# Where five early loads are queued, and a second MLP layer with batches on two column groups

## The chip, the cores and the metric

The kernel runs on one core of a Trainium2 chip. The metric is the device time of one execution in microseconds (us). Executions of one kernel agree within some 0.3%; the kernel before shows two groups of times, near 668.3 and near 669.7 us, in the same session. Every kernel is compared with runs of the kernel before in its own session. A ratio is the mean time of one kernel's fast runs over that of the kernel before's fast runs of the same rounds, so it is not quite the ratio of the medians quoted beside it.

## The reference

One decode step of a transformer block for 8 batches, width 512, bf16. The key and value caches (8 batches, 8 heads, 8192 x 128 each) are 268 MB of the 284 MB read.

```python
mod = silu(c) @ w_mod                    # six parts: sa, ca, ga, sb, cb, gb
h = layernorm(x) * (1 + ca) + sa
x = x + ga * attention(h, k_cache, v_cache, wq, wo)   # 32 query heads, 8 kv heads
h = layernorm(x) * (1 + cb) + sb
x = x + gb * (relu(h @ w1 + b1) ** 2 @ w2 + b2)       # 512 -> 1792 -> 512
```

## The kernel before

Each engine runs its instructions in the order in which the program adds them; semaphores tie engines together. The caches come in 64 units of 4 MB, K units and V units below, through a ring of four slots in SBUF. Code here and below is shortened: `...` marks a cut, and lines such as `a += b @ c` stand for one instruction. SyncE issues almost all loads. w_mod and wq borrow ring slots 2 and 3, so K units 2 and 3 wait until those are used. The first V unit (`n == NSLOT`) also waits for wo, which makes that wait stand in for one in front of wo's readers inside the batch loop.

```python
def load(n):
    ...
    dep = [released.get(s), d_wo if n == NSLOT else None]
    ...
    loaded[n] = dma("sync", s_ring[s], lambda e: e.dma_start(slot(s), src), dep)
...
# after the projections of mod and q:
load(0)
load(1)
dma("sync", s_bb, ... b1 ...); dma("sync", s_bb, ... b1 ...); d_bb = dma("sync", s_bb, ... b2 ...)
d_wo = dma("sync", s_wo, lambda e: e.dma_start(
    wo_sb[:, :, :].rearrange("p (g j) n -> p g (j n)", j=4),     # 8 runs of 4 KB per partition
    A_wo.rearrange("(g p j) n -> p g (j n)", g=8, p=128)))
load(2)
load(3)
```

The end, after the last V unit: w1 comes in two loads and w2 in four, all queued behind the last V unit. The first layer runs over k (4) and then f (14), so all 14 tiles finish with the last k. The second layer has the weights as stationary operand and 8 batch columns moving.

```python
for k in range(KT):
    ...
    for f in range(FT):          # 56 matmuls, 128x16 out
        hT_ps[f // 8][:, f % 8] += W1[k, f].T @ hbT[:, k]
# two halves: scale, add, squared relu on VectorE
for f in range(FT):
    for k in range(KT):          # 56 matmuls, 128x8 out
        yT_ps[:, k, :] += W2v[:, f, 128*k:128*(k+1)].T @ hidT[:, f, :]   # waits d_w2[f // 4]
k_y2 = vector: y2T = yT_ps * mod(5)
# four transposing matmuls of y2T (and four of x1T, the residual) into o_ps rows 0:8 and 64:72
# copy (VectorE one half, ScalarE the other), store from two queues
```

## Time and profile before

The median was 669.21 us over four runs (668.52 to 669.9), the three before the prediction included.

| in the trace of before | us |
|---|---|
| span, first to last instruction | 666.7 |
| first data packet | 1.8 |
| w_mod, wq, K0, K1, wo landed | 11.3, 21.0, 30.8, 41.1, 51.3 |
| K2, K3 landed | 61.6, 71.3 |
| four w2 loads landed | 660.17, 661.46, 662.69, 663.33 |
| store issued (SyncE) | 664.92 |

Landings here and below are the last of the 16 increments that the DMA engines give a load's semaphore. The prediction below shows the views that go with them. In a view, SPq and ACTq are the DMA issues of SyncE and ScalarE, PEld is a weight load of TensorE, and PEclk is the granted share of TensorE's clock.

### The profile page before, as it was taken

Reading aid. Unit: us, or ns where it says so; the run is one execution under the profiler, and the core shown is the slowest. Engines: PE = TensorE matmul, PEld = TensorE weight load, DVE = VectorE, ACT = ScalarE, POOL = GpSimd, SP = SyncE. Lnnn points to the kernel's source line nnn. Section 1 sums busy time; section 2 is a strip of 40 time slices with the busy share of each in tenths; the row PEclk is TensorE's granted clock in tenths of the full one; section 3 lists DMA queues with packets and bytes.
Section 4 is the critical chain, followed back from the end, with each engine's and each line's share of the span. In section 5 each row is a group of like instructions: output and inputs, shape, how many; then the busy total and the mean of one; then the engine's idle time right before and its main releaser. Section 6 shows DMA issues by size and latency. Waiting matters only on the chain.

```text
span 666.7 us, 15924 instructions
## 1 busy us (share of the span) xinstructions
PE 528.3 (79%) x7259; PEld 352.2 (53%) x7259; DVE 307.9 (46%) x587; ACT 264.3 (40%) x307; POOL 20.5 (3%) x79
## 2 busy tenths in 40 slices
PE   3494976898849987599858988499776998589887
PEld 2383732675328742477316753287424773277535
DVE  1262741466316652367415662167513673146633
ACT  2151631466115651166314661166512663146611
POOL 7400000000000000000000000000000000000000
PEclk9696998799969999699998999799997999879996
DMA  9999999999999999999999999999999999999997
GB/s 375 437 406 441 419 433 433 425 434 431 438 427 433 433 434 427 434 434 425 434 431 438 427 431 434 434 427 431 438 425 434 433 436 427 431 434 434 427 420 285
DMA packets 12189, 283.85 MB, mean 426 GB/s; under 512 B 1261, under 2 KB 1297, under 8 KB 3601
## 3 DMA queue, kind: packets, MB, share of 16 engines
q1 hardware_dynamic: 12128, 283.65, 99.3%
q8 instruction: 9, 0.15, 0.1%
q10 hardware_dynamic: 48, 0.02, 0.0%
q14 instruction: 4, 0.02, 0.0%
HBM read 283.66 MB, written 0.01 MB: 425 GB/s over the span
## 4 chain that ended last, share of the span: by engine, by line
PE 52%; DMA 38%; ACT 6%; DVE 2%; issue 1%; SPq 0%; DVEq 0%
PE PS L488 36%; DMA ring<-in_A_k_cache_dram 33%; PE PS L505 9%; ACT P_sb L582 5%; DMA ring<-in_A_v_cache_dram 4%; DMA ring<-in_A_wq_dram 2%; PE PS L636 2%; PE PS L478 1%; ACT KTb L493 1%; DVE O_sb L656 1%; PE PS L472 1%; PE PS L594 1%; DVE Pm L608 0%; PE PS L614 0%; PE PS L773 0%
## 5 line engine op out<-in xcount | busy, mean ns | idle before, releaser
L488 PE MATMUL PS<-IDENT,ring 128*128 128x128 bf16 x4096 | 267.1, 227 | 56.2 <-DMA ring<-in_A_k_cache_dram 56.2
L488 PEld LDWEIGHTS PS<-IDENT,ring 128*128 128x128 bf16 x4096 | 246.5, 102 | 104.8 <-DMA ring<-in_A_k_cache_dram 57.4
L493 ACT ACTIVATE KTb<-PS 128x1024 bf16<-128x1024 bf16 x192 | 196.5, 1024 | 236.6 <-PE PS L488 236.6
L495 DVE COPY KTb<-PS 128x1024 bf16<-128x1024 bf16 x320 | 210.0, 688 | 146.5 <-PE PS L488 144.4
L636 PE MATMUL PS<-ring,Pm 128*32 128x512 bf16 x1018 | 67.2, 409 | 24.8 <-DMA ring<-in_A_v_cache_dram 23.9
L505 PE MATMUL PS<-KTb,Qb 128*32 128x512 bf16 x1024 | 79.0, 385 | 4.5 <-ACT KTb L493 4.5
L656 DVE CAST O_sb<-PS 128x512 bf16<-128x512 f32 x31 | 21.5, 692 | 112.7 <-PE PS L636 112.7
L636 PEld LDWEIGHTS PS<-ring,Pm 128*32 128x32 bf16 x1018 | 26.5, 101 | 61.8 <-DMA ring<-in_A_v_cache_dram 33.7
L535 ACT ACTIVATE KTb<-PS 32x192 bf16<-32x192 f32 (+1 forms) x18 | 5.6, 310 | 110.0 <-PE PS L472 103.9
L582 ACT ACTIVATE P_sb<-PS,negm 128x1024 bf16<-128x1024 f32 x32 | 35.2, 1111 | 20.2 <-DVE negm L577 20.2
L478 PE MATMUL PS<-ONES 128*128 128x512 f32 x80 | 42.1, 630 | 0.0
L472 PE MATMUL PS<-IDENT 128*128 128x512 bf16 x112 | 33.4, 380 | 0.0
L594 PE MATMUL PS<-IDENT,P_sb 128*128 128x128 bf16 x256 | 19.9, 220 | 15.4 <-ACT P_sb L582 15.4
L608 DVE COPY Pm<-PS 64x512 bf16<-64x512 bf16 x48 | 20.2, 421 | 25.0 <-PE PS L594 24.5
L594 PEld LDWEIGHTS PS<-IDENT,P_sb 128*128 128x128 bf16 x256 | 14.4, 98 | 25.1 <-ACT P_sb L582 25.1
L505 PEld LDWEIGHTS PS<-KTb,Qb 128*32 128x32 bf16 x1024 | 15.4, 94 | 21.0 <-ACT KTb L493 8.5
L512 DVE TENSOR_REDUCE m<-PS 128x1 f32<-128x512 f32 x32 | 22.1, 689 | 6.6 <-PE PS L505 6.6
L660 PEld LDWEIGHTS PS<-SEL,O_sb 128*128 128x128 bf16 x124 | 5.8, 97 | 30.0 <-DVE O_sb L656 30.0
L478 PEld LDWEIGHTS PS<-ONES 128*128 128x128 f32 x80 | 12.7, 190 | 10.6 <-issue 10.6
L660 PE MATMUL PS<-SEL,O_sb 128*128 128x8 bf16 x124 | 7.8, 169 | 12.3 <-DVE O_sb L656 12.0
L472 PEld LDWEIGHTS PS<-IDENT 128*128 128x128 bf16 x112 | 9.9, 104 | 10.1 <-issue 7.2
L543 PE MATMUL PS<-wo_sb,KTb 128*32 128x512 bf16 x192 | 11.8, 380 | 3.3 <-ACT KTb L535 3.3
(134 smaller groups left out, 147.0 us busy)
## 6 DMA issues: line engine op xcount, KB each, us to landing
ring<-in_A_k_cache_dram SPq DMA_DIRECT2D x32, 4096.0 KB, 34.0
ring<-in_A_v_cache_dram SPq DMA_DIRECT2D x31, 4096.0 KB, 27.8
ring<-in_A_wq_dram SPq DMA_DIRECT2D x1, 4096.0 KB, 19.8
wo_sb<-in_A_wo_dram SPq DMA_DIRECT2D x1, 4096.0 KB, 47.3
ring<-in_w_mod_dram SPq DMA_DIRECT2D x1, 3072.0 KB, 10.5
ring<-in_A_v_cache_dram SPq DMA_DIRECT2D x1, 2048.0 KB, 22.5
ring<-in_B_w_dram SPq DMA_DIRECT2D x3, 512.0 KB, 19.2
ring<-in_B_w_dram SPq DMA_DIRECT2D x1, 1344.0 KB, 17.8
```

Source lines behind the costliest of these rows:

```text
L472: ts = [op("tensor", lambda e: e.matmul(bank(at).rearrange("p (a r) -> p a r", a=4), IDENT[:, :], rhs)) for _ in range(n)]
L478: ts = [op("tensor", lambda e: e.matmul(bank(at).rearrange("p (a r) -> p a r", a=4), ONES[:, :], rhs)) for _ in range(n)]
L488: t = op("tensor", lambda e, j=j, i=i: e.matmul(STG[j][:, i, :], src[:, 32 * k + 8 * j + i, :], IDENT[:, :], is_transpose=True), [loaded[n ...
L493: stg_free[j] = op("scalar", lambda e, j=j, dst=dst: e.activation(dst, STG[j], ACT.Copy), [t])
L495: stg_free[j] = op("vector", lambda e, j=j, dst=dst: e.tensor_copy(dst, STG[j]), [t])
L505: t = op("tensor", lambda e, hf=hf, q=q, rhs=rhs: e.matmul(PS[32 * q:32 * (q + 1), k, :], Qb[:, 2 * p + hf, :], rhs, start=(p == 0 and hf ...
L512: return op("vector", lambda e: e.tensor_reduce(m4[:, k:k + 1], bank(k), AX.X, ALU.max), [t])
L582: exps.append(op("scalar", lambda e, k=k: e.activation(P_sb[:, k, :, :, :], bank(k).rearrange("p (i x) -> p i x", i=8).unsqueeze(2).to_bro ...
L594: t = op("tensor", lambda e, k=k, i=i: e.matmul(STG[k][:, i, :], P_sb[:, k, i, :, :].rearrange("p h x -> p (h x)"), IDENT[:, :], is_transp ...
L608: done.append(op("vector", lambda e, dst=dst, frm=frm: e.tensor_copy(dst, frm), [t, k_pm]))
L636: t = op("tensor", lambda e, m=m, cg=cg, p=p, vt=vt, Obank=Obank: e.matmul(Obank[32 * cg:32 * (cg + 1), :], lhs[:, p, 32 * m:32 * m + 32], ...
L656: t = op("vector", lambda e, osb=osb, Obank=Obank: e.tensor_copy(osb, Obank), [t])
```

## The change

Its intent was to shorten the end and to relieve SyncE and GpSimd. The first layer is done for tiles 0 to 7 and then 8 to 13, so that the second can begin early. The second layer swaps its operands: the batches are stationary, 256 columns of w2 move, on two column groups of the array; the result then lies in rows as the output wants it, so the gate, the residual and the store follow without transposes. ScalarE issues five of the early loads. GpSimd builds its constants with fewer instructions.

```diff
+        for q in range(4):
+            op("vector", ... mod5[32 * q:32 * (q + 1), :] <- mod_r[96:128, 1, ...])
         load(0)
-        load(1)
-        dma("sync", s_bb, ... b1 ...)
+        load(1, "scalar")
+        dma("scalar", s_bb, ... b1 ...)          # and the other two bias loads
-        d_wo = dma("sync", s_wo, lambda e: e.dma_start(
+        d_wo = dma("scalar", s_wo, lambda e: e.dma_start(
...
+        # beside the mean: x1_ps rows 0:8 and 64:72 <- x1T transposed; later two ScalarE copies to x1_sb
-        for k in range(KT):
-            for f in range(FT):
+        for hh, (fa, fz) in enumerate(((0, 8), (8, FT))):
+            for k in range(KT):
+                for f in range(fa, fz):
...
         for f in range(FT):
-            for k in range(KT):
-                yT_ps[:, k, :], W2v[:, f, k * 128:(k + 1) * 128], hidT[:, f, :]
+            for cc in range(2):
+                y_ps[64 * cc:64 * cc + B, :], hidT[:, f, :], W2v[:, f, 256 * cc:256 * (cc + 1)],
+                    tile_position=(0, 64 * cc)
-        k_y2 = vector: y2T = yT_ps * mod(5);  transposes;  copies
+        vector: y_sb = y_ps * mod5
+        vector: out_sb = y_sb + x1_sb
...
-        # GpSimd: 7 selects for R4, 4 for R4m, 32 for SEL
+        # GpSimd: 4 selects for R4, one scaled copy for R4m, 4 for SEL
```

More of the change, by code (lines that the diff above doesn't have):

```diff
@@ L225, in bass_adaLN_cond__gqa_block_cached__dense_activation_squared_relu__decode_kernel @@
         cb1 = sb("cb1", [128, KT, B], FP32)
-        b_row = sb("b_row", [4, 512 + 128], BF16)
-        SELB = sb("SELB", [4, 4, B], BF16)
+        b_row = sb("b_row", [4, 512 + 256], BF16)
+        SELB = sb("SELB", [4, 4, 32], BF16)
         SELP = sb("SELP", [128, B], FP32)
         x1T = sb("x1T", [128, KT, B], BF16)
+        x1_sb = sb("x1_sb", [128, 256], BF16)
+        mod5 = sb("mod5", [128, 256], FP32)
         sqs = sb("sqs", [128, B], FP32)
@@ L256, in bass_adaLN_cond__gqa_block_cached__dense_activation_squared_relu__decode_kernel @@
         proj = KF[:, 4096:5120].bitcast(FP32)
-        b1_row, b2_row = b_row[:, 0:512], b_row[:, 512:640]
-        y2T = KF[:, 0:KT * B].rearrange("p (k b) -> p k b", k=KT)
+        b1_row, b2_row = b_row[:, 0:512], b_row[:, 512:768]
+        y_sb = KF[:, 5120:5376]
         rT = KF[:, 1024:1024 + 2 * FT * B].bitcast(FP32).rearrange("p (f b) -> p f b", f=FT)
@@ L301, in bass_adaLN_cond__gqa_block_cached__dense_activation_squared_relu__decode_kernel @@
         pool(lambda e: e.memset(Qmask[:], 1.0))
-        pool(lambda e: e.memset(R4m[:], 0.0))
+        pool(lambda e: e.memset(x1_sb[:], 0.0))
         pool(lambda e: e.memset(SEL[:], 0.0))
@@ L325, in bass_adaLN_cond__gqa_block_cached__dense_activation_squared_relu__decode_kernel @@
         k_pm = t
-        for d in (-96, -64, -32, 0, 32, 64, 96):
-            t = select(R4[:], [[-1, 128]], -d, 1, 1.0, NE, t)
+        for d in (0, 32, 64, 96):
+            t = select(R4[:].rearrange("p (a r) -> p a r", a=4), [[0, 4], [-1, 32]], -d, 1, 1.0, NE, t)
         t = select(Qmask[:], [[-32, 4]], 0, 1, 0.0, GE, t)
         t = select(Qmask[:], [[32, 4]], 31, -1, 0.0, GE, t)
-        for d in (0, 32, 64, 96):
-            t = select(R4m[:], [[-1, 32]], -d, 1, 0.5, NE, t)
-        for i in range(4):
-            for cg in range(4):
-                for half in range(2):
-                    t = select(SEL[:, i, 4 * half:4 * half + 4], [[-1, 4]], -(32 * cg + 8 * i + 4 * half), 1,
-                               1.0, NE, t)
+        t = pool(lambda e: e.tensor_scalar(R4m[:], R4[:, 0:32], 0.5, None, ALU.mult), [t])
+        for cg in range(4):
+            t = select(SEL[:], [[-8, 4], [-1, 8]], -32 * cg, 1, 1.0, NE, t)
         t = pool(lambda e: e.memset(SELP[:], 0.0), [t])
@@ L342, in bass_adaLN_cond__gqa_block_cached__dense_activation_squared_relu__decode_kernel @@
         t = select(PERM[:], [[-1, 4], [0, 4], [-4, 32]], 0, 1, 1.0, NE, t)
-        t = select(SELB[:], [[-1, 4], [0, B]], 0, 1, 1.0, NE, t)
+        t = select(SELB[:], [[-1, 4], [0, 32]], 0, 1, 1.0, NE, t)
         t = pool(lambda e: e.memset(oTn[:], 0.0), [t])
@@ L353, in bass_adaLN_cond__gqa_block_cached__dense_activation_squared_relu__decode_kernel, with load @@
         F2 = FT - 2
-        def load(n):
+        def load(n, eng="sync"):
             kv, b, p = units[n]
@@ L368, in load @@
             else:
-                loaded[n] = dma("sync", s_ring[s], lambda e: e.dma_start(slot(s), src), dep)
+                loaded[n] = dma(eng, s_ring[s], lambda e: e.dma_start(slot(s), src), dep)
         k_sig = op("scalar", lambda e: e.activation(sig, c_sb, ACT.Sigmoid), [d_c])
@@ L449, in bass_adaLN_cond__gqa_block_cached__dense_activation_squared_relu__decode_kernel @@
         k_cb1 = op("vector", lambda e: e.tensor_scalar(cb1[:], mod(4), 1.0, None, ALU.add))
+        for q in range(4):
+            op("vector", lambda e, q=q: e.tensor_copy(
+                mod5[32 * q:32 * (q + 1), :], mod_r[96:128, 1, 256 * (q // 2):256 * (q // 2 + 1)]), [k_mr1])
         stg_free = [k_modT, None, None, k_QTm]
@@ L453, in bass_adaLN_cond__gqa_block_cached__dense_activation_squared_relu__decode_kernel @@
         load(0)
-        load(1)
-        dma("sync", s_bb, lambda e: e.dma_start(
+        load(1, "scalar")
+        dma("scalar", s_bb, lambda e: e.dma_start(
             b1_row[0:3, :], B_b1[0:128 * F2].rearrange("(o f) -> o f", o=3)), [k_brow])
-        dma("sync", s_bb, lambda e: e.dma_start(
+        dma("scalar", s_bb, lambda e: e.dma_start(
             b1_row[3:4, 0:256], B_b1[128 * F2:F].rearrange("(o f) -> o f", o=1)))
-        d_bb = dma("sync", s_bb, lambda e: e.dma_start(b2_row, B_b2.rearrange("(o f) -> o f", o=4)))
-        d_wo = dma("sync", s_wo, lambda e: e.dma_start(
+        d_bb = dma("scalar", s_bb, lambda e: e.dma_start(b2_row[0:4:2, :], B_b2.rearrange("(o f) -> o f", o=2)))
+        d_wo = dma("scalar", s_wo, lambda e: e.dma_start(
             wo_sb[:, :, :].rearrange("p (g j) n -> p g (j n)", j=4),
@@ L516, in bass_adaLN_cond__gqa_block_cached__dense_activation_squared_relu__decode_kernel @@
         hT_ps = [bank(i)[:, 0:16 * n].rearrange("p (f a b) -> p f a b", f=n, a=2) for i, n in enumerate((8, FT - 8))]
-        yT_ps = bank(2)[:, 0:KT * B].rearrange("p (k b) -> p k b", k=KT)
+        y_ps = bank(2)[:, 0:256]
         def permute(pP, q0, q1, dst, deps, fill, then=None):
@@ L706, in bass_adaLN_cond__gqa_block_cached__dense_activation_squared_relu__decode_kernel @@
                             op("tensor", lambda e, hh=min(hh, 1), f0=f0 + j, j=j, n=n, a=a, z=z: e.matmul(
-                                hT_ps[hh][:, f0:f0 + 4 * (z - a - 1) + 1:4, 1, :], brow(j, n), SELB[:, a:z, :],
+                                hT_ps[hh][:, f0:f0 + 4 * (z - a - 1) + 1:4, 1, :], brow(j, n), SELB[:, a:z, 0:B],
                                 start=(f0 == 0), stop=False, skip_group_check=True), [d_bb, s_bank_free[min(hh, 1)]])
                     op("tensor", lambda e: e.matmul(
-                        yT_ps, b2_row, SELB[:, :, :], start=True, stop=False, skip_group_check=True),
+                        y_ps, SELB[:, :, :].rearrange("o a r -> o (a r)"), b2_row, start=True, stop=False, skip_group_check=True),
                         [s_bank_free[2]])
@@ L741, in bass_adaLN_cond__gqa_block_cached__dense_activation_squared_relu__decode_kernel @@
                                                     stop=(k == KT - 1)), [k_x1])
+        x1_ps = bank(7)[:, 0:256]
+        for cc in range(2):
+            rows = slice(64 * cc, 64 * cc + B)
+            for k in range(2):
+                t1 = op("tensor", lambda e, rows=rows, k=k, cc=cc: e.matmul(
+                    x1_ps[rows, 128 * k:128 * (k + 1)], x1T[:, 2 * cc + k, :], IDENT[:, :],
+                    tile_position=(0, 64 * cc)), [k_x1])
         bc = lambda ap: ap.unsqueeze(1).to_broadcast([128, KT, B])
@@ L751, in bass_adaLN_cond__gqa_block_cached__dense_activation_squared_relu__decode_kernel @@
         rsb = lambda n: rstd2[:].unsqueeze(1).to_broadcast([128, n, B])
-        for k in range(KT):
-            if k == KT - 1:
-                t = op("tensor", lambda e: e.matmul(var_ps, ONESM[:, :], sqs[:]), [k_sqs])
-                t = op("scalar", lambda e: e.activation(std2[:], var_ps, ACT.Sqrt, bias=epst[:, 0:1]), [t])
-                k_rstd = op("vector", lambda e: e.reciprocal(rstd2[:], std2[:]), [t])
-            for f in range(FT):
-                t = op("tensor", lambda e, f=f, k=k: e.matmul(
-                    hT_ps[f // 8][:, f % 8, :, :], wcol(k, f), hbT[:, k, :, :], start=False, stop=(k == KT - 1),
-                    skip_group_check=True), [k_hb, k_sb, d_w1[k // (KT - 1)]])
-                if k == KT - 1 and f in (7, FT - 1):
-                    hh = f // 8
-                    fs = slice(8 * hh, f + 1)
-                    t = op("vector", lambda e, hh=hh, fs=fs: e.tensor_tensor(
-                        rT[:, fs, :], hT_ps[hh][:, :, 0, :], rsb(fs.stop - fs.start), ALU.mult), [t, k_rstd])
-                    t = op("vector", lambda e, hh=hh, fs=fs: e.tensor_tensor(
-                        rT[:, fs, :], rT[:, fs, :], hT_ps[hh][:, :, 1, :], ALU.add), [t])
-                    k_sq.append(op("vector", lambda e, fs=fs: e.scalar_tensor_tensor(
-                        hidT[:, fs, :], rT[:, fs, :], 0.0, rT[:, fs, :], ALU.max, ALU.mult), [t]))
@@ L770, in bass_adaLN_cond__gqa_block_cached__dense_activation_squared_relu__decode_kernel @@
-        o_ps = bank(4)[:, 0:256]
-        for f in range(FT):
-            for k in range(KT):
-                t = op("tensor", lambda e, f=f, k=k: e.matmul(
-                    yT_ps[:, k, :], W2v[:, f, k * 128:(k + 1) * 128], hidT[:, f, :],
-                    start=False, stop=(f == FT - 1), skip_group_check=True), [k_sq[f // 8], d_w2[f // 4]])
-        for cc in range(2):
-            for k in range(2):
-                op("tensor", lambda e, k=k, cc=cc: e.matmul(
-                    o_ps[64 * cc:64 * cc + B, 128 * k:128 * (k + 1)], x1T[:, 2 * cc + k, :], IDENT[:, :],
-                    start=(k == 0), stop=False, tile_position=(0, 64 * cc), skip_group_check=True), [k_x1])
@@ L781, in bass_adaLN_cond__gqa_block_cached__dense_activation_squared_relu__decode_kernel @@
-        k_y2 = op("vector", lambda e: e.tensor_tensor(y2T, yT_ps, mod(5), ALU.mult), [t])
-        outf = out.rearrange("b s d -> (b s) d")
-        d_o = []
-        for cc in (1, 0):
-            for k in range(2):
-                t = op("tensor", lambda e, k=k, cc=cc: e.matmul(
-                    o_ps[64 * cc:64 * cc + B, 128 * k:128 * (k + 1)], y2T[:, 2 * cc + k, :], IDENT[:, :],
-                    start=False, stop=(k == 1), tile_position=(0, 64 * cc), skip_group_check=True), [k_y2])
-            rows = slice(64 * cc, 64 * cc + B)
-            if cc == 0:
-                t = op("vector", lambda e, rows=rows: e.tensor_copy(out_sb[rows, :], o_ps[rows, :]), [t])
-            else:
-                t = op("scalar", lambda e, rows=rows: e.activation(out_sb[rows, :], o_ps[rows, :], ACT.Copy), [t])
-            d_o.append(dma(("sync", "scalar")[cc], s_out[cc], lambda e, cc=cc, rows=rows: e.dma_start(
-                outf[:, 256 * cc:256 * (cc + 1)], out_sb[rows, :]), [t]))
+        for hh, (fa, fz) in enumerate(((0, 8), (8, FT))):
+            for k in range(KT):
+                if (hh, k) == (0, 2):
+                    t = op("tensor", lambda e: e.matmul(var_ps, ONESM[:, :], sqs[:]), [k_sqs])
+                    t = op("scalar", lambda e: e.activation(std2[:], var_ps, ACT.Sqrt, bias=epst[:, 0:1]), [t])
+                    k_rstd = op("vector", lambda e: e.reciprocal(rstd2[:], std2[:]), [t])
+                    for rows in (slice(0, B), slice(64, 64 + B)):
+                        k_res = op("scalar", lambda e, rows=rows: e.activation(
+                            x1_sb[rows, :], x1_ps[rows, :], ACT.Copy), [t1])
+                for f in range(fa, fz):
+                    t = op("tensor", lambda e, f=f, k=k: e.matmul(
+                        hT_ps[f // 8][:, f % 8, :, :], wcol(k, f), hbT[:, k, :, :], start=False, stop=(k == KT - 1),
+                        skip_group_check=True), [k_hb, k_sb, d_w1[k // (KT - 1)]])
+            fs = slice(fa, fz)
+            t = op("vector", lambda e, hh=hh, fs=fs: e.tensor_tensor(
+                rT[:, fs, :], hT_ps[hh][:, :, 0, :], rsb(fs.stop - fs.start), ALU.mult), [t, k_rstd])
+            t = op("vector", lambda e, hh=hh, fs=fs: e.tensor_tensor(
+                rT[:, fs, :], rT[:, fs, :], hT_ps[hh][:, :, 1, :], ALU.add), [t])
+            k_sq.append(op("vector", lambda e, fs=fs: e.scalar_tensor_tensor(
+                hidT[:, fs, :], rT[:, fs, :], 0.0, rT[:, fs, :], ALU.max, ALU.mult), [t]))
@@ new lines, in bass_adaLN_cond__gqa_block_cached__dense_activation_squared_relu__decode_kernel @@
+        for f in range(FT):
+            for cc in range(2):
+                t = op("tensor", lambda e, f=f, cc=cc: e.matmul(
+                    y_ps[64 * cc:64 * cc + B, :], hidT[:, f, :], W2v[:, f, 256 * cc:256 * (cc + 1)],
+                    start=False, stop=(f == FT - 1), tile_position=(0, 64 * cc), skip_group_check=True),
+                    [k_sq[f // 8], d_w2[f // 4]])
+        t = op("vector", lambda e: e.tensor_tensor(y_sb, y_ps, mod5[:], ALU.mult), [t])
+        t = op("vector", lambda e: e.tensor_tensor(out_sb, y_sb, x1_sb[:], ALU.add), [t, k_res])
@@ L796, in bass_adaLN_cond__gqa_block_cached__dense_activation_squared_relu__decode_kernel @@
+        outf = out.rearrange("b s d -> (b s) d")
+        d_o = [dma(eng, s_out[cc], lambda e, cc=cc: e.dma_start(
+            outf[:, 256 * cc:256 * (cc + 1)], out_sb[64 * cc:64 * cc + B, :]), [t])
+            for cc, eng in enumerate(("sync", "scalar"))]
         Pg.wait("sync", d_o)
```

## The prediction

> **What bounds the kernel now.** I read the page first, for what is busy all the time:
>
> ```profile
> DMA  9999999999999999999999999999999999999997
> GB/s 375 437 406 441 419 433 433 425 434 431 438 427 433 433 434 427 434 434 425 434 431 438 427 431 434 434 427 431 438 425 434 433 436 427 431 434 434 427 420 285
> ```
>
> All 16 DMA engines are busy from the first slice to the last, at some 430 GB/s: 283.65 MB have to pass. No compute engine is full (PE 79%, DVE 46%). In the packet records of the trace 15 or more packets are in flight for 658 of the 666.7 us, and none for only 2.8 us, nearly all of it before the first packet (1.8 us) and after the last. So the time is three terms: 1.8 us until data flows, one unbroken stream, and what follows its last byte. A change can move the time only by tearing a hole into the stream or by altering the end.
>
> The second view is the timeline, SyncE's early issues and then the tail. Columns are start, length, engine, line, operation.
>
> ```profile
> 0.80 0.39 SPq L287 DMA_DIRECT2D ring<-in_w_mod_dram  x1
> 1.25 0.42 SPq L289 DMA_DIRECT2D ring<-in_A_wq_dram  x1
> 1.72 1.26 SPq L369 DMA_DIRECT2D ring<-in_A_k_cache_dram  x2
> 4.00 0.40 SPq L460 DMA_DIRECT2D wo_sb<-in_A_wo_dram  x1
> 14.86 23.69 SPq L369 DMA_DIRECT2D ring<-in_A_k_cache_dram  x2
> 51.38 31.83 SPq L369 DMA_DIRECT2D ring<-in_A_v_cache_dram  x4
> ```
>
> By 4.4 us five big loads (w_mod, wq, two K units, wo) stand in one queue, and they land in that order: 11.3, 21.0, 30.8, 41.1 and 51.3 us. The first V load waits for wo (51.38, just after it landed), but two more K units stand behind wo and keep the engines busy until 71. The wait costs nothing.
>
> ```profile
> 660.88 0.23 DVE L764 TENSOR_TENSOR KTb<-PS,rstd 128x64 f32<-128x64 f32 x1
> 661.68 2.06 PE L773 MATMUL PS<-KTb,ring 128*128 128x8 bf16 x56 [1.00 <-DVE KTb L768]
> 663.78 0.19 DVE L781 TENSOR_TENSOR KTb<-PS,modT 128x32 bf16<-128x32 f32 x1 [1.56 <-PE PS L773]
> 664.03 0.38 PE L786 MATMUL PS<-IDENT,KTb 128*8 128x128 bf16 x4
> 664.49 0.41 DVE L791 CAST KTb<-PS 8x256 bf16<-8x256 f32 x1 [0.51 <-PE PS L786]
> 664.92 0.31 SPq L794 DMA_DIRECT2D out_dram<-KTb  x1
> ```
>
> The chain of waits puts this tail down to PE and DVE. The landings say otherwise. The four w2 loads, by the semaphore events, land at 660.17, 661.46, 662.69 and 663.33 us, and the second-layer matmuls stop and start with them: tiles 8 to 11 begin at 662.83, the last two at 663.37. So the weights, not the first layer, set when the second layer ends.
>
> ```profile
> L682 SPq DMA_DIRECT2D ring<-in_B_w_dram x4: 885/1444/5533, 641.0 to 649.9; - x4
> DMA to landing us min/median/max: 13.5/17.0/19.2
> ```
>
> The last is issued at 649.9 and lands 13.5 us later: 663.4. After it come 8 matmuls, a multiply, 4 transposes, a copy and the store. The granted clock is 0.5 from 656.2 us to the end.
>
> **What the Trainium skill says.** *DMA: Bandwidth & Descriptors*, "Queues, rings and completion order": SP and ACT each own one ring on each of the same 16 engines, and an engine goes round-robin between rings by packet. The trace agrees. The load of x (ScalarE's queue, 1 KB packets), issued at 1.44 among 24 KB packets of w_mod, starts its packets only at 5.4 to 6.8 us, behind about four; and in all eight pairs (matched in order of time) its 4-byte completion packet starts 0.95 us after the data packet, about one 24 KB packet (0.92 to 1.0 us), against 0.04 us for the load of c, while nothing competes. Small packets pay one large one per turn. The same page, "Issuing engines are not separate DMA queues": a second issuer saves issue time alone. *TensorEngine Tiling (Array Packing)*, "Key Properties": column tiles run in parallel. This trace agrees: 32 matmuls of 512 columns on four column groups took 3.60 us at clock 0.53, 8 rounds of 0.45 us, and 24 of which eight used two groups took 3.42, again 8 rounds. *VectorE: DVE Perf Modes* (table of caps by operand): a tensor_tensor with a PSUM operand runs at 1x. Here 128x512 from PSUM took 0.69 us and 128x64 0.23, so some 0.43 for 256 columns.
>
> **The change part by part.**
> *Set-up on GpSimd.* It loses 3 of 7 wide selects, 4 small and 28 of 32 tiny ones (29 of them took 9.48 us). GpSimd now ends at 29.4 us and the first K unit lands at 30.8, so the 10 us saved are hidden. Four 32x256 copies on DVE (mod5) are added near 27 us, some 1.5 us, about the same place and hidden. Worth 0.
>
> *Five loads on ScalarE.* A queue is in program order: in the new order these loads stand behind the activation that copies q, which runs at 24.81 to 25.41. So K unit 1, the biases and wo go out at about 25.4 to 28 us instead of 2 to 4.4. Meanwhile SyncE holds w_mod, wq, K0 (to 30), K2 (issued at 14.86 with room in the queue) and K3 (about 24.8). No hole there. But now two rings compete. Per engine a 4 MB K unit is 8 packets of 32 KB (1.217 us each), wo is 64 of 4 KB (0.164 each). K1 starts behind about four packets, near 31, then alternates with K2: both end near 31 + 16 x 1.217 = 50.5. Then K3 alternates with wo, one packet each: 7 to 8 turns x 1.38 = 10 us, so K3 ends near 61 with only 8 of wo's 64 packets moved. The other 56 take 9.2 us: wo's data ends near 70, **last of all**. The first V load, which has to wait for it, and all loads behind it in SyncE's queue find the stream empty. The hole: 0.42 us from last data to landing (x: 7.75 to 8.13), 0.08 to issue, 1.04 to first packets (0.80 to 1.84 at the start), some 0.8 as first packets are slow (1.5 to 2.4 us against 0.92 later), and part of the spread of the engines' landings (1.7 us), since the slowest gates all: 2.3 + 0.3 = **+2.6 us**. PE has K1 at 51 instead of 41, but ends K3 near 81 as now near 83; slots 1 and 2 are released by about 70.
>
> *First layer half by half.* Lets the second layer begin at about 660.8 (32 of 56 matmuls, 1.2 us after 658.28, then three DVE operations of 0.77) instead of 661.68. That is 0.9 us gained which the w2 landings take back: tiles 8 to 11 still begin at 662.83. Worth 0.
>
> *Second layer with batches on two column groups.* 56 matmuls of 8 columns (32 ns each) become 28 of 256. At half clock a pair takes 256/1.2 GHz = 0.213 us (scaled from the 0.45 us round). Tiles 8 to 11: 662.83 + 0.85 = 663.68; the last two + 0.43, and 0.1 to 0.15 until the result is there: 664.2, against 663.78 before. **+0.45 us**. At full clock it would be near 663.75: 0.
>
> *Gate and residual.* Removed after the matmuls: multiply, transposes back and copy, 663.78 to 664.90 = 1.12 us. Added: a 128x256 multiply (0.43) and an add (0.43 or less) with a gap of 0.03: 0.89. **-0.25 us**. The residual's transposes move into PE's idle time near 657.9, and their two copies to ScalarE's near 660.
>
> Sum: 0 + 2.6 + 0 + 0.45 - 0.25 = +2.8 us.
>
> **Rivals.**
> *(a) wo comes in time.* If the rings share by bytes, wo lands near 66, before K3 ends near 70, and there is no hole: 669.8. Against it are the x packets above. For it: x shows one packet per turn, not a long run.
> *(b) The end gains after all.* If tiles and half clock are not as supposed, the tail may save up to 0.8 us as the author wanted: 669 with (a). Against it are the w2 landings.
> *(c) The column groups serialize,* or the weight load of each pair shows: +0.85 us or more behind the last two landings, 673 to 674. Against it are the two rounds above.
> *(d) ScalarE blocks in issuing wo,* as SyncE's load at 14.86 blocked until 37.5 behind wo. It would stall the copies of K0, which has slack; 0 to +0.5.
>
> **Range and chances.** The hole I hold 85% likely. With it 672.4 with 0.9 either way; without it 669.3 to 670.2. Weighted I say **672.2 us, 670.2 to 673.8**. Two per cent are 13 us, and neither the stream's bytes nor its rate change: same 0.97, slower 0.02, faster 0.01.
>
> **What would show it.** In the new profile: wo landing near 71, after K3, and the next V issue right after; a dip of the DMA share near 70 to 73; K1 landing near 50. In the tail: second layer starting some 0.9 us earlier against the last landing, but ending 0.8 us behind it, its matmuls pausing for w2. The prediction is wrong if wo lands before K3, if the DMA share has no dip, or if the matmuls of the second layer take 1.7 us or more per four tiles.

## The result, and the profile after

The changed kernel takes 672.9 us (672.61 to 673.1, 4 runs) against 669.21: ratio 1.0055, 95% interval 1.0037 to 1.0072. It is 3.7 us slower, inside the two per cent that count as the same, but clear of noise.

The page of the changed kernel, rows of DMA share and rate:

```profile
DMA  9999899999999999999999999999999999999996
GB/s 374 433 426 412 336 430 436 433 435 431 424 431 437 433 433 426 430 433 433 437 431 422 431 437 433 435 428 426 433 435 435 431 430 426 435 433 435 428 416 263
```

One slice, the fifth (67 to 84 us), has fallen from 419 to 336 GB/s. Nothing else of that size has changed in the middle. The timeline of the changed kernel, SyncE's issues and then ScalarE's early ones, shows what stands around it:

```profile
1.73 23.16 SPq L367 DMA_DIRECT2D ring<-in_A_k_cache_dram  x3
71.40 8.97 SPq L367 DMA_DIRECT2D ring<-in_A_v_cache_dram  x4
...
24.57 0.60 ACT L430 ACTIVATE KTb<-PS 128x512 bf16<-128x512 f32 x1 [8.76 <-PE PS L400]
24.58 0.38 ACTq L367 DMA_DIRECT2D ring<-in_A_k_cache_dram  x1
26.37 0.40 ACTq L461 DMA_DIRECT2D wo_sb<-in_A_wo_dram  x1
```

SyncE's first V load went out at 51.38 before; now it goes out at 71.40. wo, issued at 26.37, landed at 71.32, last of all; K1, K2 and K3 had landed at 49.62, 50.83 and 62.84. SyncE's waits, before and then after, name it (columns: total us, times, longest):

```profile
SPq L116 <- DMA wo_sb<-in_A_wo_dram: 12.7, 1, 12.7
```

```profile
SPq L116 <- DMA wo_sb<-in_A_wo_dram: 46.4, 1, 46.4
```

The wait before cost nothing, since two K units were still queued behind wo. The stretches around 70 us, first before and then after (length, busy us and count of PE, PEld, DVE, ACT, POOL, then clock, DMA share, GB/s), show that the longer one does. A packet is counted whole in the stretch in which it starts, so a share can pass 1:

```profile
68.00:70.00 2.00, 2.00 (x37) 1.63 (x30) 1.09 (x3) 1.48 (x2) 0.00 (x0) 1.00 0.87 369
70.00:72.00 2.00, 2.00 (x37) 1.47 (x33) 1.30 (x3) 1.03 (x2) 0.00 (x0) 1.00 0.97 410
72.00:74.00 2.00, 2.00 (x36) 1.47 (x34) 1.29 (x3) 1.52 (x2) 0.00 (x0) 1.00 1.21 524
```

```profile
68.00:70.00 2.00, 2.00 (x40) 1.88 (x40) 1.30 (x3) 1.05 (x2) 0.00 (x0) 1.00 0.58 229
70.00:72.00 2.00, 2.00 (x37) 1.59 (x30) 1.10 (x3) 1.48 (x2) 0.00 (x0) 1.00 0.03 12
72.00:74.00 2.00, 2.00 (x36) 1.47 (x34) 1.30 (x3) 1.03 (x2) 0.00 (x0) 1.00 0.98 270
```

PE is full in both, and at full clock: no compute engine shows the loss. Only the DMA share does. Summed over the packet records of the two load queues between 65 and 80 us, the 16 engines stand still for 3.35 us on average after and 0.12 before. This stretch is called the hole below.

The end of the changed kernel, in the timeline:

```profile
664.08 0.23 DVE L774 TENSOR_TENSOR KTb<-PS,rstd 128x64 f32<-128x64 f32 x1
664.87 3.43 PE L782 MATMUL PS<-ring,KTb 128*8 128x256 bf16 x28 [0.16 <-DVE KTb L778]
666.82 0.97 PEld L782 LDWEIGHTS PS<-ring,KTb 128*8 128x8 bf16 x12 [0.58 <-issue]
668.34 0.42 DVE L786 TENSOR_TENSOR KTb<-PS,mod 128x256 bf16<-128x256 f32 x1 [2.91 <-PE PS L782]
668.80 0.29 DVE L787 TENSOR_TENSOR KTb<-KTb,x_sb 128x256 bf16<-128x256 bf16 x1
669.12 0.37 SPq L789 DMA_DIRECT2D out_dram<-KTb  x1
```

The four w2 loads landed at 664.19, 665.48, 666.72 and 667.35. Each event is best read against the last of them, since the hole has shifted everything. The second layer starts 2.48 us ahead of it (1.65 before), so the first layer by halves does what it was meant to. But the matmuls pause until the third load has landed, and run on to 0.95 us behind the last (0.42 before). The store is issued 1.77 us behind it, 1.59 before.

### The profile page after: what moved, and what is told of

Its sections match the earlier page's. It is cut to its first block, busy times and chain, and to the rows that moved or that the text cites. A ratio compares the mean times of both kernels' runs of the same rounds, so it can differ in the third digit from the quotient of the medians.

```text
span 671.4 us, 15797 instructions
## 1 busy us (share of the span) xinstructions
PE 530.9 (79%) x7227; PEld 353.1 (53%) x7227; DVE 309.9 (46%) x591; ACT 264.7 (39%) x308; POOL 14.7 (2%) x45
## 4 chain that ended last, share of the span: by engine, by line
PE 54%; DMA 37%; ACT 6%; DVE 2%; issue 1%; SPq 0%; DVEq 0%
PE PS L489 37%; DMA ring<-in_A_k_cache_dram 30%; PE PS L506 10%; ACT P_sb L583 5%; DMA ring<-in_A_v_cache_dram 4%; DMA ring<-in_A_wq_dram 3%; PE PS L637 2%; PE PS L479 1%; ACT KTb L494 1%; DVE O_sb L657 1%; PE PS L473 1%; PE PS L595 1%; PE PS L400 1%; PE PS L782 0%; DVE Pm L609 0%
## 5 line engine op out<-in xcount | busy, mean ns | idle before, releaser
L494 ACT ACTIVATE KTb<-PS 128x1024 bf16<-128x1024 bf16 x192 | 196.7, 1024 | 230.3 <-PE PS L489 230.3
```

What stands on the lines that cost most here:

```text
L494: stg_free[j] = op("scalar", lambda e, j=j, dst=dst: e.activation(dst, STG[j], ACT.Copy), [t])
```

## The experiments

Eight kernels, all with correct results. The first four of the table's eight were timed in five rounds in one session (kernel before: 668.28, nine runs), the other four in three rounds in another (669.44, seven runs).

| kernel | median us | ratio to before (95%) | wo landed | idle DMA, 65 to 80 us |
|---|---|---|---|---|
| changed | 672.90 | 1.0055 (1.0037 to 1.0072) | 71.3 | 3.35 |
| changed, loads back | 668.95 | 1.0010 (0.9996 to 1.0024) | 51.9 | 0.12 |
| changed, wo alone back | 668.75 | 1.0003 (0.9989 to 1.0017) | 51.2 | 0.12 |
| loads back, four groups | 669.07 | 1.0006 (0.9992 to 1.0019) | 51.8 | 0.07 |
| before, halves only | 668.49 | 0.9998 (0.9984 to 1.0011) | 51.1 | 0.12 |
| before, five loads moved | 672.52 | 1.0046 (1.0029 to 1.0063) | 71.2 | 3.35 |
| before, wo alone moved | 672.21 | 1.0042 (1.0025 to 1.0058) | 71.2 | 3.19 |
| changed, loads issued at the start | 672.86 | 1.0051 (1.0034 to 1.0068) | 71.3 | 3.34 |
| changed, wait moved to the third V load | 672.84 | 1.0053 (1.0036 to 1.0070) | 90.6 | 0.12 (3.08 from 80 to 100) |

A packet is one piece that one DMA engine moves, as the trace records it. My theory, H: two queues share each DMA engine by turns of one packet, so wo with its 4 KB packets is starved by units with 32 KB packets, lands last, and the V load that waits for it finds the stream empty. The rivals: T, the new second layer costs the time; K, the late second K unit does, by delaying PE and the slots; L, the loads are merely issued too late.

**The five loads, undone and alone.** In the changed kernel:

```diff
-        load(1, "scalar")
+        load(1)
-        dma("scalar", s_bb, ...)     # three, and d_wo
+        dma("sync", s_bb, ...)
```

> The changed kernel with its five early loads (second K unit, three bias rows, wo) back on SyncE in the old place; everything else of the change stays. Theory H (the hole: wo lands last, about 70 us, because two rings alternate packet by packet, and the first V load waits for it): wo lands near 51 again, the 3.2 us of idle DMA engine time between 65 and 80 us go to 0.1, and the time is the kernel before's plus the tail's 0.2: 669.4 us, ratio to before 1.000 (0.999 to 1.001). Rival T (the second layer with 256 columns at half clock costs the time): stays near 672, ratio 1.004.

It came to 1.0010: the hole is gone (0.12 us idle, wo at 51.9) and so is the loss, but for at most the tail. The opposite edit, in the kernel before:

> The kernel before with only the five loads moved to ScalarE, all else old. Theory H: the whole loss is here: wo lands near 71 us after the fourth K unit, 3.2 us of idle DMA engine time near 70, 672.4 us, ratio 1.0048. Rival T (the tail): ratio 1.000.

It came to 1.0046. The two add up to the whole change: 0.0010 + 0.0046 against 0.0055. T falls as the cause of the loss; a small cost of the tail, up to 0.0024 by the interval of the first, stays possible.

**wo alone, undone and alone.** In the changed kernel and, turned round, in the kernel before:

```diff
-        d_wo = dma("scalar", s_wo, ...
+        d_wo = dma("sync", s_wo, ...
```

> The changed kernel with wo alone moved back to SyncE's queue, behind the first K unit; the second K unit and the bias rows stay late on ScalarE. Theory H: wo lands by about 52 us, no hole near 70, 669.4 us, ratio 1.000 though the second K unit still lands late, at 41 to 50. Rival K (the late second K unit delays PE and with it all slot releases): stays at 672.5 to 673, ratio 1.005.

> The kernel before with only the load of wo moved to ScalarE, which comes to it at about 25 us. Theory H: three K units stand on SyncE's queue, wo's small packets get one turn to each of theirs, wo lands last near 70 to 71 and the hole is the same: 672.4 us, ratio 1.0048. Rival K (the late second K unit): it is early here, so no loss, ratio 1.000.

With wo back the ratio is 1.0003, with the second K unit and the biases still on ScalarE and that unit issued at 24.60; it landed at 41.98, though, nearly as early as before. With wo alone moved, the loss is there in full, 1.0042, though the second K unit landed at 42.7. In the two kernels SyncE's first V issues stand as far apart as in before and after (first wo back, then wo alone moved):

```profile
51.25 31.79 SPq L367 DMA_DIRECT2D ring<-in_A_v_cache_dram  x4
```

```profile
71.32 4.27 SPq L369 DMA_DIRECT2D ring<-in_A_v_cache_dram  x4
```

So one load in one place is the whole cause of the hole, and K falls as its explanation: the second K unit is early in the kernel that loses. That a K unit at 50 us would be harmless by itself was not run; in neither of these two did it come that late.

**Late, or on the other queue?** The five loads stay on ScalarE but stand ahead of its first activation:

```diff
+        load(1, "scalar")            # and the biases and wo, as they were
         k_sig = op("scalar", lambda e: e.activation(sig, c_sb, ACT.Sigmoid), [d_c])
...
         load(0)
-        load(1, "scalar")            # and the biases and wo
         load(2)
```

> The changed kernel with the five loads still on ScalarE but issued at the very start, before its first activation. Theory H (two rings by turns of one packet, 4 KB against 32 KB): w_mod is held up by the second K unit to 18 or 20 us, wo is starved by wq and the K units and still lands last, 66 to 71 us; the hole stays for the most part: 671.5 to 673, ratio 1.003 to 1.006. Rival L (only the late issue at 25 us does harm): no hole, ratio 1.000.

wo was issued at 4.47 us, nearly as early as in the kernel before (4.00), and landed at 71.32; w_mod at 18.8 instead of 11.3, wq at 31.9. Ratio 1.0051. L falls: with these two queues, issuing early does not help.

The packet records confirm the turns in numbers. In this kernel 439 of wo's 1024 packets had started by 60 us: 27 per engine, one for each of the 8 large packets of wq, of K0 and of K2, and three of K3. In the kernel with wo alone moved it was 416, 26 per engine; in the changed kernel, where wo comes behind the second K unit, 150, some 9 per engine. There, from 50 to 58 us, 94 packets of wo started beside 93 of SyncE's K units, though each of the latter is eight times as large.

One more rival is that ScalarE's queue as such is served less. The second K unit in the changed kernel speaks against it: it was on that queue too, with packets of 32 KB, and from 32 to 46 us 89 of them started beside 89 on SyncE's queue. A load of wo in larger packets, which would test the size alone, was not run.

**What if the load does not wait?** The wait for wo moves to the third V load, whose landing still comes ahead of wo's first reader:

```diff
-            dep = [released.get(s), d_wo if n == NSLOT else None]
+            dep = [released.get(s), d_wo if n == NSLOT + 2 else None]
```

> The changed kernel with the wait for wo moved from the first V load of the first batch to the third (wo is first read after the third has landed). Theory H: nothing is idle near 70 any more, but the first two V units join SyncE's queue and starve wo for 16 more turns: it lands last at 88 to 91 us, and the third V load then finds the stream empty: the hole moves to near 90 and the time stays, 672 to 673, ratio 1.004 to 1.006. Rival: if wo gets a fair share of bytes once the wait is gone, it lands by 80, no hole, ratio 1.000.

The ratio is 1.0053 and the hole has moved along: SyncE issued the first V unit at 43.96, wo, starved for 16 more turns, landed at 90.59, and the stretches around 90 us of this kernel look like those around 70 of the changed one:

```profile
86.00:88.00 2.00, 1.13 (x16) 0.79 (x14) 1.20 (x3) 2.00 (x5) 0.00 (x0) 1.00 1.00 399
88.00:90.00 2.00, 1.45 (x18) 1.11 (x19) 1.07 (x4) 1.68 (x4) 0.00 (x0) 1.00 0.38 154
90.00:92.00 2.00, 1.69 (x15) 0.61 (x16) 0.91 (x4) 0.63 (x2) 0.00 (x0) 1.00 0.84 231
```

As long as the other queue has large packets, wo is served one small packet per turn, and whoever waits for it waits until the other queue is dry. Wait and starvation together make the hole.

**The halves alone.** The kernel before with the changed first layer and nothing else:

> The kernel before with only the first layer by halves; second layer, output transposes and loads as before. My step: the second layer starts some 0.9 us earlier against the last weight landing, but tiles 8 to 11 still begin 0.13 us after the third w2 load landed and the last two after the fourth, so the time stays: ratio 1.000 (0.9990 to 1.0005). Rival: the first layer is on the path and 0.8 us are saved, ratio 0.9988.

Ratio 0.9998. The second layer of this kernel, in the timeline:

```profile
660.80 1.23 PE L772 MATMUL PS<-KTb,ring 128*128 128x8 bf16 x32 [0.18 <-DVE KTb L767]
662.76 0.93 PE L772 MATMUL PS<-KTb,ring 128*128 128x8 bf16 x24 [0.73 <-DMA ring<-in_B_w_dram]
664.87 0.31 SPq L793 DMA_DIRECT2D out_dram<-KTb  x1
```

It starts 2.46 us ahead of the last w2 landing (663.26) instead of 1.65, does 32 matmuls, and then waits 0.73 us for the third w2 load. The store is issued 1.61 us behind the last landing, against 1.59. What was gained went into waiting for the weights.

**A tail with four column groups.** With the loads back, the second layer on four groups of 128 columns, tried as a version that might beat both kernels:

```diff
-            for cc in range(2):      # y_ps[64*cc: +8, 0:256] on column group 64*cc
+            for cc in range(4):      # y_ps[32*cc: +8, 0:128] on column group 32*cc
...
-        two stores of 8x256, one per queue
+        four stores of 8x128, two per queue
```

> Loads on SyncE as in the kernel before, first layer by halves, and the second layer on four column groups of 128 columns instead of two of 256; gate and residual on 128x128; four stores of 2 KB, two per queue. If column groups run side by side, each pair of tiles after the last weights takes half: second layer ends 0.3 to 0.4 us earlier against the last landing than in the changed kernel, gate and add together 0.50 instead of 0.71, one more store issue in each queue +0.3: in all 0.2 to 0.4 below the run with the loads back, 669.0 us, ratio 0.9990 to 0.9998. If groups serialize: nothing gained in the matmuls, ratio 1.000 or more.

Its tail, in the timeline; the last w2 load landed at 663.14:

```profile
663.63 0.29 DVE L783 TENSOR_TENSOR KTb<-PS,mod 128x128 bf16<-128x128 f32 x1 [2.22 <-PE PS L779]
663.95 0.22 DVE L784 TENSOR_TENSOR KTb<-KTb,x_sb 128x128 bf16<-128x128 bf16 x1
664.20 0.65 SPq L786 DMA_DIRECT2D out_dram<-KTb  x2
664.21 0.97 ACTq L786 DMA_DIRECT2D out_dram<-KTb  x2
```

The groups do run side by side. The gate begins 0.49 us behind the last landing (0.99 in the run with the loads back) and the first store is issued 1.06 us behind it (1.76). But a second store stands in each queue: ScalarE's two issues take 0.97 us, and the last store landed 3.62 us behind the weights against 3.19 with two stores and 2.94 in the kernel before. The time, 669.07 beside 668.95, is not better: I expected 0.2 to 0.4 us and had given the second issue 0.3, without counting that its landing comes later as well. No version tried beats the kernel before.

## Why the prediction was right or wrong

672.2 was predicted, 672.9 measured, inside the range of 670.2 to 673.8. The forecast started from 669.61, the median of the three runs then known, so its sum of +2.8 stands against a measured +3.7. That start lay 0.4 above the later median of four, 669.21, and made up that much of the shortfall; this part of the closeness is luck.

**What bounds it, right.** The stream has no slack: loads alone cost 1.0046 with every compute engine as it was, and 0.8 us of earlier second layer brought 0.9998.

**The five loads, mechanism right, size short.** The forecast of the landings held: K1 and K2 near 50.5 (49.6 and 50.8), K3 near 61 (62.8), wo near 71 (71.3), the V issue right behind it (71.40). The first K unit came later, at 33.3 instead of 30.8, which the forecast had not seen and which cost nothing visible. The idle term was +2.6 us; the experiment with the loads alone shows 0.0046, or 3.1 us, with an interval of 1.9 to 4.2, so the time alone does not refute 2.6. The traces do: the last w2 load landed at 666.80 to 667.36 us in the five kernels with a hole and at 663.14 to 663.35 in the five without, at least 3.4 us apart. The term that was too small is "part of the spread of the engines' landings", which I put at 0.3. In the changed kernel wo's 16 engines landed at 69.72 on average and the slowest at 71.32, so the average engine stood still 1.60 us for the slowest before the wait was even over. The other terms of that sum: last data to landing 0.43 (0.42 predicted), issue 0.08 (0.08), first packets 0.95 to 1.8 after the issue began, 1.19 on average (1.04). These four make 3.3 us, and 3.35 was counted. The first 16 packets then took 1.55 to 2.25 us each, on average some 0.67 above the usual 1.22 (0.8). All five sum to 4.0 for the average engine, as the landings have it. Why the times show 3.1 stays open; the traces without a hole come from runs of 668.45 to 669.07 us, while the timed runs of the kernel before reach 670.36.

**Arbitration, right.** The rule of the Trainium skill, *DMA: Bandwidth & Descriptors*, "Queues, rings and completion order", that an engine goes round its queues packet by packet, carried the forecast, and the counts of 150, 416 and 439 packets agree with turns of one packet. Rival (a), shares by bytes, is out: it had wo in near 66, before the fourth K unit, and wo came at 71.3, after that unit's 62.8. In the run with the later wait it would have brought wo in by 80, and it came at 90.6.

**Halves, right.** Worth 0, shown alone.

**The second layer, right in sign and nearly in size.** +0.45 predicted for the matmuls; the layer's end moved from 0.42 to 0.95 us behind the last landing, +0.53. It ran at clock 0.5 to the end, as assumed: six pairs from 666.82 to 668.30, 0.213 us each plus 0.2. Gate and residual: from the layer's end to the store 1.17 before and 0.82 after, -0.35 against -0.25 predicted. The multiply took 0.42 (0.43), the add 0.29 and not 0.43. Its operands are bf16 in SBUF, for which *VectorE: DVE Perf Modes* of the Trainium skill gives tensor_tensor a doubled rate in "The perf-mode tier table"; I had read that table for the PSUM operand only. The trace fits in direction, 0.29 against 0.42 for as many elements, though it is not half; what else differs between the two was not separated. Net +0.18 us at the store; the run with the loads back is slower by 0.0010 with an interval that includes 0, so the time itself neither confirms nor denies it. Rival (b), a tail that saves up to 0.8 us, does not appear: with the loads back the store is issued 1.76 us behind the last weights, against 1.59 in the kernel before.

**GpSimd, argued only.** No run changes the constants alone. GpSimd ends them at 29.5 us before and 18.8 after, and the first K unit lands behind that in both, at 30.8 and 33.3.

**Rivals (c) and (d).** Column groups did not serialize. ScalarE's issue of wo took 0.40 us, and its next wait, 7.06 us at 35.28, was for PE.

**Slips in the working.** None changes the argument. The stated chances (85% for 672.4, else 669.3 to 670.2) weigh out at 672.0, not 672.2. For the halves, 658.28 + 1.2 + 0.77 is 660.25, not 660.8; the variance's two matmuls, 0.57 us, stand between and are not named. A pair's 0.213 us is half of 0.427, the distance of the weight loads in those rounds (21.54, 21.97, 22.40 us, clock 0.50); half of 0.45 would be 0.225. From 7.75 to 8.13 is 0.38, not 0.42. No packet is in flight for 4.9 us, not 2.8: 1.8 at the start and 3.1 at the end. The 0.69 us for 128x512 from PSUM is a copy, not a tensor_tensor, yet the 0.43 read off it held (0.42).

## What to carry to other kernels

Before a load is moved to another queue, ask what is queued beside it and who waits for it: here two queues shared the DMA engines by turns of one packet, so the load with 4 KB packets, issued at 4.5 or at 26 us, landed at 71.3 either way, when the queue with 32 KB packets had run dry. The stream forgave a late load but not a wait at its head: one wait cost 3.1 us of a 669 us kernel, and moving the wait only moved the hole. And where the last weights arrive at the end of a saturated stream, read each instruction against the last landing; in this kernel what ended before it gained nothing (0.9998 for 0.8 us).

## What the Trainium skill lacked or had wrong

- *DMA: Bandwidth & Descriptors*, "Queues, rings and completion order", speaks of packets of 9 to 17 descriptors. Here a turn was one recorded packet, 32 KB on one queue against 4 KB on the other; it does not say that shares of bandwidth follow the packet size. Measured: 94 packets of wo beside 93 of the K units from 50 to 58 us of the changed kernel; 150 of wo's 1024 packets started by 60 us there, 439 with wo issued at 4.47 us.
- The same page, "Issuing engines are not separate DMA queues", says that issuing from several engines only saves issue time. It lacks that this can cost: one 4 MB load moved to the second queue made the kernel 0.42% slower (669.44 to 672.21 us).
- The same page has figures for the start and the completion of a single DMA, but I found no page that says what an empty stream costs in all: here 3.35 us of standing still on average per engine, of which 1.60 is the wait for the slowest engine's landing; the first packets then took 1.55 to 2.25 us instead of 1.22.
